# Moving raw weight words, r loads and weight conversion in the first third of an RWKV-7 and hard-swish FFN kernel

## The chip, the cores and the metric

One core of a Trainium2 chip runs the whole program. The metric is the device time of one execution in microseconds (us). PE is the matrix engine, DVE the vector engine, ACT the scalar engine, POOL GpSimd, SP the engine that here only issues DMAs. Each engine works through its own instructions in the order in which the program gives them, and waits where an operand is not ready.

## The reference

Two blocks follow each other. The first is a recurrence over 768 time steps, for 4 batches and 8 heads, with a 40x40 state per head:

```python
y[:, :, t] = einsum('bhd,bhde->bhe', r_t, state)
Sa = einsum('bhde,bhe->bhd', state, a_t)
state = state * w_t[:, :, None, :] - einsum('bhd,bhe->bhde', Sa, b_t) + einsum('bhd,bhe->bhde', v_t, k_t)
```

The second is a feed-forward network (FFN) on the 3072 tokens, each of the 8 x 40 = 320 numbers of y: `h = x @ w_in` (320 to 2048), `g = h * clip(h + 3, 0, 6) / 6`, `out = g @ w_out` (2048 to 320). Inputs of the recurrence are float32. The two weights are float64.

## The kernel before

**The recurrence by blocks.** Time is cut into 12 blocks of 64 steps, batches into two pairs; a block of a pair is a *unit*, 24 in all (`NK`), worked in the order of time, the two pairs in turn. Four units (`NU`) form a *group*. The preparation of a unit (`prepare`) needs no state: products of the decays w (DVE scan L456, reciprocals L467 and L482, copies on POOL L468 to L471), transposes of w, a, b, k on PE (L413), scaled copies, score matmuls masked on DVE (L431, L440), the matrix F of a and b (L505), and KBt on POOL (L549). Then a group's triangular matrices are inverted together (`invert`): a transpose (L607), thirty pairs of a product and an addition on DVE (L619, L625), each needing the one before, and two transposes out (L628, L633); `third_block` (L653 to L680) completes the inverse in `tinv`, the matrix that the diff calls T (128 x 32 x 64 floats, 8 KB in each partition). `step` then carries the state through a unit in named stages: RT and VT (turns of r and v on PE, copied out by ACT, L697 and L729), the scaling of the state (L703 on POOL, L705 on DVE), R (L718, L723), S (L740, L745), U and UT (L756, L777), C and H (score matmuls L431 and masks L440), rS (L793), sn (L811; the state is updated on DVE at L818), y (L834, L846), yg on POOL (L849), and `move` and `move2`, DMAs on SP that lay yg out as the FFN's input xt (L863, L868). Results of PE go through five PSUM banks used in turn, so a stage waits until the bank of five turns ago was read.

**The weights.** PE works in float32, so float64 weights are converted on the chip, in 20 pieces of 1024 raw 32-bit words a partition (`load_weights`). A piece is five DVE instructions (L292, L313, L318, L300, L305) and two of ACT (L294 after L292, L321 after L318). Each `next(weights)` emits one step of this, so what another part of the program asks for sets how densely conversion stands in DVE's order. Raw words need room until they are converted: `raw_homes` lists a home for each piece, in the order of use, and after which piece's conversion a home is free. Homes now are the two halves of the tile `raw` (a, b), two parts of `wout` (c, d) and of `win` (e, f) that are not yet written, and, once the first inversion is over, its tiles `fb`, `tt` and `x`. `limit` says how many pieces may be loaded so far: 2 at the start, 4 and then 12 in the first preparation, all 20 from round 3 on (below). Loads are DMAs on SP (L273).

**The FFN.** For each unit there are two jobs, one for each half of the hidden size. `expand` has 16 matmuls at L914 and 8 at L919 into two PSUM banks `h`, then ACT (L924) and DVE (L925) make two tiles `gt`; `contract` of the job before has 8 matmuls at L938. (Each of these is two matmul records in the trace.) A job is 9 *pieces*, 5 of expand and 4 of contract, and `pieces(n)` emits n of them. A job may be emitted when its xt is there and enough weights are converted (`available`: 10 pieces for the first job of the first two units, else 20).

**The order.** It is written out by hand. First the group 0 is prepared (`by_twos`). Then comes the first inversion, in a loop that lays conversion steps and the first stages of units 0 and 1 between its instructions. Then follow 24 rounds t in which the units 0 to 3 each take one stage a round, beginning at rounds 0, 2, 4 and 10:

```python
for i in range(NU):
    if 0 <= t - begins[i] < len(mine[i]) and mine[i][t - begins[i]]:
        run(chains[i], weight=2.5)
```

`run` emits a stage; at each point where the stage waits for PE, it adds `weight` steps of conversion. From t = 16 on, the preparation of group 1 (`second_group`) runs in the same rounds, with FFN pieces between; the rounds 9 to 15 have one piece each (`FIRST = 9`). After these come 18 turns with 1.25 pieces and the second inversion's instructions. From there the units follow in four blocks each, with FFN pieces at fixed rates, and the rest of the FFN comes last.

**Queues.** `fetch` loads a unit's input, on SP unless an engine is named (L396 for r and v, L399 for the others). `fetch("R", i + 1, ...)` stands after r's turn in the stage RT; ACT issues it for i = 0, 1, 2, SP from then on. ACT also issues the loads of w, a, b and k of unit 5, in rounds 12, 17 and 18.

Of the kernel before, what the change touches and what calls it, by code (L numbers as in the profile page):

```python
# [10 lines left out]
U32 = mybir.dt.uint32  # L11
# [12 lines left out]
def _ap(ap, extra, dims):  # L24

    return bass.AP(tensor=ap.tensor, offset=ap.offset + extra, ap=[list(ap.ap[0])] + dims)
# [3 lines left out]
def kernel(  # L30
# [42 lines left out]
    nc = tc.nc  # L73
# [4 lines left out]
    NU = 2 * NP  # L78
# [84 lines left out]
    def seconds():  # L163
        t = inv.tile([P, 2, H, SLOT], F32, name="WA1", tag="x", bufs=1)
        for i, name in enumerate("WA"):
            others[name] = padded(t[:, i], name)
# [18 lines left out]
    for i in range(3):  # L185
        t = const.tile([P, H, BL], F32, name=f"score{i}")
# [10 lines left out]
    tinv = const.tile([P, NH, BL], F32, name="tinv")  # L197
# [3 lines left out]
    for p in range(NP):  # L201
        t = const.tile([P, 2, NPR, SLOT], F32, name=f"state{p}")
        nc.vector.memset(t[:], 0.0)
        state.append(t)
        t = const.tile([P, 2, NPR], F32, name=f"last{p}")
# [15 lines left out]
    WC = 256  # L221
    PIECES = 20
    converted = [0]
    phase = [0]
    limit, refill = [2], []

    def raw_homes():


        raws = inv.tile([P, NH, BL], F32, name="raw", tag="F", bufs=2)  # L230
        raws = raws[:].rearrange("p h t -> p (h t)").bitcast(U32)
        places = [raws[:, n * 4 * WC:(n + 1) * 4 * WC] for n in range(2)]
        for j in (NJ // 4, 3 * NJ // 4):
            places.append(wout[:, j:j + NJ // 4, :].rearrange("p j m -> p (j m)")[:, 0:4 * WC].bitcast(U32))
        places = [x.rearrange("p (n c t) -> p n c t", n=2, t=2) for x in places]
        for c in (DFF // 4, 3 * DFF // 4):
            x = win[:, :, c:c + 2 * WC].bitcast(U32)
            places.append(x.rearrange("p n (c t) -> p n c t", t=2))
        a, b, c, d, e, f = places
        order = [a, b, c, d, e, f, a, b, c, d, a, b, "fb", "tt", "x", d, a, b, "fb", "tt"]  # L240
        free = [None] * 6 + [0, 1, 2, 3, 6, 7, None, None, None, 9, 10, 11, 12, 13]
        left = {}
        for n, (x, before) in enumerate(zip(order, free)):
            if isinstance(x, str):
                if x not in left:
                    left[x] = inv.tile([P, L, L], F32, name=f"raw_{x}", tag=x)
                x = left[x][:].rearrange("p t s -> p (t s)").bitcast(U32)
                x = x.rearrange("p (n c t) -> p n c t", n=2, t=2)
            yield x, before
# [129 lines left out]
    def fetch(name, i, engine=None):  # L379

        if i is None or i >= NK:
            return
        x, crossed = {"W": (w, 0), "A": (a, 0), "B": (b, 0), "K": (k, 0), "R": (r, 1),
                      "V": (v, 1)}[name]
        if name == "V":
            t = values[i % AHEAD]
        else:
            t = (others if i < 2 * NU and i % 2 and name != "R" else inputs)[name]
        g, p = names[i]
        engine = engine or nc.sync  # L390
        for q in range(2):
            y = x[2 * p + q, :, g * BL:(g + 1) * BL, :]
            rows = slice(q * BL, (q + 1) * BL)
            if crossed:
                for s in range(2):
                    engine.dma_start(out=t[rows, 4 * s:4 * s + 4, 0:D],  # L396
                                     in_=y[s::2].rearrange("h t e -> t h e"))
            else:
                engine.dma_start(out=t[rows, :, 0:D], in_=y.rearrange("h t e -> t h e"))  # L399
        data[i][name + "N"] = t  # L400
# [8 lines left out]
    def turn_pairs(x):  # L409

        o = ps_any([P, NPR, P])
        for n in range(NPR):
            nc.tensor.transpose(out=o[:, n, :],  # L413
                                in_=x[:, 2 * n:2 * n + 2, :].rearrange("p s e -> p (s e)"),
                                identity=ident[:])
        return o

    def turned(name):
        return tmp.tile([P, NPR, P], F32, name=name, tag="turned", bufs=5)
# [168 lines left out]
    def in_turn(stages, order):  # L588

        for name in order:  # L590
            yield from stages[name]()
            shared[0] = None
            yield DONE
# [91 lines left out]
    def step(i):  # L685

        n, o = i % NU, data[i]
        g, p = names[i]
# [4 lines left out]
        def s_RT():  # L693
            x = turn_pairs(o["RN"])
            yield PE
            m["RT"] = turned("RT")
            nc.scalar.activation(out=m["RT"][:], in_=x[:], func=AF.Copy)  # L697
            fetch("R", i + 1, nc.scalar if i < NU - 1 else None)
            if fresh:
                nc.gpsimd.tensor_copy(last_dec[p][:], dec[:, 1])  # L700
                return
            scale = tmp.tile([P, 2, NPR], F32, name="scale", bufs=2)
            nc.gpsimd.tensor_tensor(out=scale[:], in0=last_dec[p][:], in1=dec[:, 0], op=ALU.mult)  # L703
            nc.gpsimd.tensor_copy(last_dec[p][:], dec[:, 1])
            nc.vector.tensor_tensor(out=st[:, :, :, 0:D], in0=st[:, :, :, 0:D],  # L705
                                    in1=_ap(scale[:], 0, [[NPR, 2], [1, NPR], [0, D]]), op=ALU.mult)
# [264 lines left out]
    def pieces(n):  # L971

        owed[0] += n
        while owed[0] >= 1:
            owed[0] -= 1
            if not next(stream):
                owed[0] = 0.0

    def aside(n, weight=0):

        for _ in range(n):
            if side and next(side[0], side) is side:
                side.popleft()
            due[0] += weight
            while due[0] >= 1:
                due[0] -= 1
                next(weights, None)

    def run(stage, steps=0, weight=0, mixed=0):

        for at in stage:
            if at == DONE:
                return
            aside(steps, mixed)
            due[0] += weight
            while due[0] >= 1:
                due[0] -= 1
                next(weights, None)
# [11 lines left out]

    STAGES = 9

    RFETCH, EARLY, FIRST, MIXED = 8, 5, 9, 1 / 3
    TWOS = 14

    def by_twos(first, steps, mixed, rate, fill={}):


        chains = [by_stages(first + i, prepared(first + i)) for i in range(NU)]
        for t in range(TWOS):  # L1020

            order = [0, 1] if t < STAGES else []
            order += [2, 3] if t > 5 else []
            if t == 3:
                order = [2, 3, 0, 1]
            for i in order:
                run(chains[i], steps if t > 10 else 0, fill.get(t, 0), mixed)
                pieces(rate / 2)
            if t == 10:
                side.append(invert(group_F[-1], third, first == 0))  # L1030
            yield
# [4 lines left out]
    for name in "WABK":  # L1036
        for i, engine in enumerate((nc.sync, nc.scalar if name == "W" else nc.sync)):
            fetch(name, i, engine)
    nc.gpsimd.memset(tinv[:], 0.0)
    for t, _ in enumerate(by_twos(0, 4, MIXED, 0, {5: 1, 6: 1, 10: 1})):  # L1040
        if t == 0:
            next(weights)
# [10 lines left out]
    stages = [step(i) for i in range(NU)]  # L1053
    chains = [in_turn(stages[0], ["RT", "VT", "C", "R"]), in_turn(stages[1], ["RT", "VT", "C"])]
    early = deque(chains[i] for i in (0, 0, 1, 1, 0, 1, 0))
    n = 0
    while not third:
        aside(1)
        if not third:
            n += 1  # L1060
            if n % 3 == 1:
                next(weights, None)
            if n % EARLY == 0 and early:
                run(early.popleft())
    assert not early
    while phase[0] in (1, 2, 3):
        next(weights)
    firsts = [third_block(*third[-1], n, True) for n in (0, 2)]
# [18 lines left out]
    chains = [in_turn(stages[i], filter(None, mine[i])) for i in range(NU)]  # L1087
    for t in range(LAST + OWN):
        if t in (1, 3):
            run(firsts[1])  # L1090
        if t == 3:
            limit[0] = PIECES
        for i in range(NU):
            if 0 <= t - begins[i] < len(mine[i]) and mine[i][t - begins[i]]:
                run(chains[i], weight=2.5)
        if t == LAST + 2:
            seconds()
            for name in "WA":
                fetch(name, NU + 1, nc.scalar)
            third.clear()  # L1100
            second_group = by_twos(NU, 3, 0, 1.25)
        if t in (LAST + 7, LAST + 8):

            name = "BK"[t > LAST + 7]
            others[name] = second(name)
            fetch(name, NU + 1, nc.scalar)
        if t >= LAST + 6:
            next(second_group)
        elif t >= FIRST:
            pieces(1)  # L1110
    for _ in weights:
        pass
    for _ in second_group:
# [146 lines left out]
```

## Time and profile before

| | us |
|---|---|
| median of 7 runs | 860.75 |
| lowest and highest | 859.24, 861.36 |
| profiled execution, its own time | 860.93 |
| its span | 859.2 |
| PE busy | 779.5 (91%) |
| PE weight loads busy | 665.9 (78%) |
| DVE busy | 532.1 (62%) |
| ACT busy | 310.8 (36%) |
| POOL busy | 155.9 (18%) |

Busy time is the sum of the stretches in which an engine has an instruction under way; the span is from the first instruction to the last. An engine's share of the whole span says little here, as the stages differ: the preparation and inversion of group 0 fill the first 83 us, the 24 rounds reach to about 191, and from then on PE works nearly without a gap. A wait is put down to the instruction or DMA that ended last before it.

### The profile page before, as it was taken

The numbers are of one execution on the slowest core, as the hardware profiler recorded it, in microseconds if no ns is written. First come the engines' busy times: TensorE is split into PE (matmuls) and PEld (weight loads), VectorE is DVE, ScalarE is ACT, GpSimd is POOL, SyncE is SP. The second block draws the span as 40 slices with busy tenths as digits, with TensorE's granted clock in tenths as the row PEclk, the third lists the DMA queues.
The fourth block names the chain that finished last, engine by engine and source line by source line (L and its number), as shares of the span: only waits on it lengthen the run. The fifth ranks groups of instructions, "written<-read, shape, count | busy, mean of one in ns | idle before, by whom it ended". The sixth has DMA issues, their size and how long they took to land.

```text
span 859.2 us, 34883 instructions
## 1 busy us (share of the span) xinstructions
PE 779.5 (91%) x15480; PEld 665.9 (78%) x15480; DVE 532.1 (62%) x1032; ACT 310.8 (36%) x756; POOL 155.9 (18%) x307
## 2 busy tenths in 40 slices
PE   4723886798999989999999999999999999999998
PEld 3623775686888878888888888888888888888886
DVE  6988797968855569834599553797446774221211
ACT  1323653232354433454423534334353324222211
POOL 4222310212121130220221222113112202000000
PEclk9655578998999998999999999999999999999999
DMA  7571453331123240322232233222132101100000
GB/s 137 86 184 50 111 143 69 57 60 31 30 51 60 48 68 17 62 45 48 45 50 40 44 57 54 46 43 40 37 57 44 26 19 27 27 19 16 14 18 16
DMA packets 174326, 45.00 MB, mean 52 GB/s; under 512 B 157408, under 2 KB 172768, under 8 KB 174176
## 3 DMA queue, kind: packets, MB, share of 16 engines
q1 hardware_dynamic: 165632, 41.46, 25.2%
q8 instruction: 122, 2.00, 1.0%
q10 hardware_dynamic: 8544, 1.31, 1.0%
q14 instruction: 28, 0.23, 0.1%
HBM read 34.08 MB, written 3.93 MB: 44 GB/s over the span
## 4 chain that ended last, share of the span: by engine, by line
PE 79%; DVE 11%; DMA 3%; issue 2%; ACT 2%; SPq 2%; POOL 1%; ACTq 0%; DVEq 0%
PE o L938 25%; PE h L914 20%; PE any L413 6%; PE h L919 6%; PE any L431 3%; PE any L811 3%; PE any L834 3%; PE any L653 2%; PE any L672 2%; DVE prod L619 2%; PE any L756 2%; PE any L718 1%; PE any L576 1%; DVE x L625 1%; SPq L399 1%
## 5 line engine op out<-in xcount | busy, mean ns | idle before, releaser
L938 PE MATMUL o<-wout,gt 128*128 128x320 f32 x768 | 233.0, 450 | 0.0
L914 PE MATMUL h<-xt,win 128*128 128x128 f32 x1536 | 195.1, 281 | 4.9 <-DVE gt L925 4.9
L914 PEld LDWEIGHTS h<-xt,win 128*128 128x128 f32 x1536 | 183.6, 194 | 12.9 <-DVE gt L925 5.0
L938 PEld LDWEIGHTS o<-wout,gt 128*128 128x128 f32 x768 | 141.6, 193 | 55.9 <-issue 2.6
L925 DVE SCALAR_TENSOR_TENSOR gt<-gt,h 128x512 f32<-128x512 f32 x96 | 61.3, 680 | 97.6 <-ACT gt L924 97.6
L924 ACT ACTIVATE gt<-h,three 128x512 f32<-128x512 f32 x96 | 60.7, 683 | 131.5 <-PE h L919 129.0
L849 POOL TENSOR_TENSOR yg<-ys,gam 128x512 f32<-128x512 f32 x24 | 41.4, 1727 | 237.1 <-DVE ys L846 141.0
L619 DVE TENSOR_TENSOR prod<-x 128x30 f32<-128x30 f32 (+9 forms) x180 | 65.8, 365 | 13.6 <-POOL x L610 8.1
L625 DVE TENSOR_TENSOR x<-x,prod 128x30 f32<-128x30 f32 (+9 forms) x180 | 64.3, 357 | 5.3
L549 POOL TENSOR_TENSOR KBt<-K,rgt 128x320 f32<-128x320 f32 x24 | 21.2, 885 | 213.0 <-ACT rgt L541 197.8
L919 PE MATMUL h<-xt,win 64*128 64x128 f32 x768 | 55.8, 285 | 0.0
L440 DVE COPY_PREDICATED score<-mask,any 128x256 f32<-128x256 int32 x143 | 53.1, 435 | 3.9 <-PE any L431 3.9
L919 PEld LDWEIGHTS h<-xt,win 64*128 64x128 f32 x768 | 46.6, 187 | 4.5 <-issue 0.3
L467 DVE RECIPROCAL gam<-prods 128x256 f32<-128x256 f32 x24 | 41.4, 1740 | 13.5 <-POOL yg L849 13.2
L846 DVE TENSOR_TENSOR ys<-any,ys 128x256 f32<-128x256 f32 x44 | 16.6, 419 | 49.6 <-PE any L576 32.3
L482 DVE RECIPROCAL rgam<-prods 128x256 f32<-128x256 f32 x24 | 41.8, 1741 | 0.0
L456 DVE TENSOR_TENSOR_SCAN prods<-wm,start 128x528 f32<-128x528 f32 x24 | 30.1, 1254 | 18.8 <-ACT wm L453 17.1
L697 ACT ACTIVATE RT<-any 128x512 f32<-128x512 f32 x24 | 14.3, 594 | 70.3 <-PE any L413 70.2
L818 DVE TENSOR_TENSOR state<-any,state 128x160 f32<-128x160 f32 x48 | 13.2, 316 | 40.3 <-PE any L431 40.1
L582 ACT ACTIVATE EV<-any 64x160 f32<-64x160 f32 x92 | 24.8, 295 | 33.5 <-PE any L576 19.5
L834 PE MATMUL any<-score,KBt 64*64 64x64 f32 x1536 | 31.0, 229 | 1.7 <-DVE RR L723 0.9
L834 PEld LDWEIGHTS any<-score,KBt 64*64 64x64 f32 x1536 | 27.1, 141 | 6.8 <-issue 3.7
(179 smaller groups left out, 1148.1 us busy)
## 6 DMA issues: line engine op xcount, KB each, us to landing
V<-in_v_dram SPq DMA_DIRECT2D x96, 40.0 KB
out_dram<-ob SPq DMA_DIRECT2D x48, 80.0 KB
B<-in_b_dram SPq DMA_DIRECT2D x46, 80.0 KB
K<-in_k_dram SPq DMA_DIRECT2D x46, 80.0 KB
R<-in_r_dram SPq DMA_DIRECT2D x84, 40.0 KB
W<-in_w_dram SPq DMA_DIRECT2D x40, 80.0 KB
A<-in_a_dram SPq DMA_DIRECT2D x40, 80.0 KB
xt<-yg SPq DMA_DIRECT2D x72, 40.0 KB
```

The source lines that it names most:

```text
L413: nc.tensor.transpose(out=o[:, n, :], in_=x[:, 2 * n:2 * n + 2, :].rearrange("p s e -> p (s e)"), identity=ident[:])
L440: nc.vector.copy_predicated(out=x[:, 4 * i:4 * i + 4, :], mask=mask4, data=o[i])
L467: nc.vector.reciprocal(gv[:, :, 0:HB], o["prods"][:, :, 0, 1:HB + 1][:, :, ::-1])
L482: nc.vector.reciprocal(rv[:, :, HB:BL], o["prods"][:, :, 1, 1:HB + 1])
L619: nc.vector.tensor_tensor(out=pv, in0=_ap(x[:], (i + 1) * L + i, [[L, n], [0, i]]), in1=_ap(x[:], i * L, [[0, n], [1, i]]), op=ALU.mult,)
L625: nc.vector.tensor_tensor(out=rest, in0=rest, in1=pv, op=ALU.add)
L834: nc.tensor.matmul(out=y[q][half(s), pr, :], lhsT=o[name][half(q), h * D:h * D + SLOT], rhs=m[name][half(q), 4 * rs + 2 * s + j, :], start ...
L914: nc.tensor.matmul(out=hp[c][:, i, :], lhsT=win[:, t, j * P:(j + 1) * P], rhs=xt[:, t, :], start=(t == 0 and i == 0), stop=False)
L919: nc.tensor.matmul(out=hp[c][:, i, :], lhsT=win2[half(c), (j0 + i) * P:(j0 + i + 1) * P], rhs=xt[half(c), 2, :], start=False, stop=(i == N ...
L924: nc.scalar.activation(out=gt[:], in_=hp[c][:], func=AF.Relu, bias=three[:], scale=1.0)
L925: nc.vector.scalar_tensor_tensor(out=gt[:], in0=gt[:], scalar=6.0, in1=hp[c][:], op0=ALU.min, op1=ALU.mult)
L938: nc.tensor.matmul(out=op[:], lhsT=gts[c][:, n, :], rhs=wout[:, c * HJ + r * NQ + n, :], start=((split or r == 0) and c == 0 and n == 0), ...
```

## The change

It has five parts:

- The first two pieces' raw words get new homes, g and h, the two halves of T (`tinv`). The memset that clears T moves from the start to the loop of the first inversion, after the second piece is converted. The order of homes and the points at which they come free change with that, and 13 pieces instead of 12 may be loaded before the rounds.
- r of units 2 and 3, and w, a, b and k of unit 5, are loaded by SP instead of ACT. r of unit 1 stays on ACT.
- In the rounds t < 10 a wait on PE brings 1.5 steps of conversion instead of 2.5; from t = 10 on it brings 3.
- `FIRST` becomes 10: rounds 10 to 15 have FFN pieces, not rounds 9 to 15.
- These rounds have two pieces each instead of one.

```diff
         for c in (DFF // 4, 3 * DFF // 4):
             x = win[:, :, c:c + 2 * WC].bitcast(U32)
             places.append(x.rearrange("p n (c t) -> p n c t", t=2))
-        a, b, c, d, e, f = places
-        order = [a, b, c, d, e, f, a, b, c, d, a, b, "fb", "tt", "x", d, a, b, "fb", "tt"]
-        free = [None] * 6 + [0, 1, 2, 3, 6, 7, None, None, None, 9, 10, 11, 12, 13]
+        x = tinv[:].rearrange("p h t -> p (h t)").bitcast(U32)
+        for n in range(2):
+            y = x[:, n * 4 * WC:(n + 1) * 4 * WC]
+            places.append(y.rearrange("p (n c t) -> p n c t", n=2, t=2))
+        a, b, c, d, e, f, g, h = places
+        order = [g, h, a, b, c, d, e, f, a, b, c, d, "x", "fb", "tt", a, b, "fb", "tt", a]
+        free = [None] * 8 + [2, 3, 4, 5, None, None, None, 8, 9, 13, 14, 15]
...
-            fetch("R", i + 1, nc.scalar if i < NU - 1 else None)
+            fetch("R", i + 1, nc.scalar if i == 0 else None)
...
-    RFETCH, EARLY, FIRST, MIXED = 8, 5, 9, 1 / 3
+    RFETCH, EARLY, FIRST, MIXED = 8, 5, 10, 1 / 3
...
-    nc.gpsimd.memset(tinv[:], 0.0)
...
-    n = 0
+    n, cleared = 0, []
     while not third:
         aside(1)
         if not third:
             n += 1
             if n % 3 == 1:
                 next(weights, None)
+            if converted[0] == 2 and not cleared:
+                cleared.append(nc.gpsimd.memset(tinv[:], 0.0))
             if n % EARLY == 0 and early:
                 run(early.popleft())
-    assert not early
+    assert not early and cleared
+    limit[0] = 13
...
-                run(chains[i], weight=2.5)
+                run(chains[i], weight=1.5 if t < FIRST else 3)
         if t == LAST + 2:
             seconds()
             for name in "WA":
-                fetch(name, NU + 1, nc.scalar)
+                fetch(name, NU + 1)
...
-            fetch(name, NU + 1, nc.scalar)
+            fetch(name, NU + 1)
         if t >= LAST + 6:
             next(second_group)
         elif t >= FIRST:
-            pieces(1)
+            pieces(2)
```

## The prediction

> **What bounds the kernel now.** I read the slices of the page first. The columns are 40 equal parts of the span, 21.5 us each.
>
> ```profile
> span 859.2 us, 34883 instructions
> PE   4723886798999989999999999999999999999998
> DVE  6988797968855569834599553797446774221211
> PEclk9655578998999998999999999999999999999999
> ```
>
> Rows are PE and DVE busy in tenths and the granted PE clock. From slice 9 on PE is full at full clock; before that DVE is the fuller engine and PE runs slowly. Nothing after about 200 us can be gained except PE work that was done before. The windows show the stages (us, then busy time of PE, PEld, DVE, ACT, POOL, then clock, DMA share and GB/s):
>
> ```profile
> 82.00:103.00 21.00, 18.41 (x585) 16.84 (x580) 14.31 (x25) 14.40 (x35) 10.01 (x19) 0.58 0.28 69
> 103.00:117.00 14.00, 9.89 (x208) 8.43 (x208) 11.18 (x26) 6.47 (x12) 0.18 (x1) 0.62 0.76 185
> 117.00:157.00 40.00, 28.23 (x568) 24.31 (x567) 32.70 (x55) 17.68 (x38) 7.73 (x16) 0.84 0.40 89
> 157.00:191.00 34.00, 32.34 (x636) 26.62 (x637) 25.29 (x35) 8.93 (x26) 6.38 (x13) 0.95 0.32 54
> 400.00:800.00 400.00, 400.00 (x8172) 342.85 (x8172) 229.29 (x473) 147.52 (x359) 69.38 (x124) 1.00 0.21 39
> ```
>
> From 82 us (end of the first inversion) to 117 PE idles 6.7 us, from 117 to 157 11.8, from 157 to 191 1.7, and none from 400 to 800. So the change is worth what it takes from the 18.5 us of PE idle between 82 and 157, plus the FFN work that it puts there. The waits of 82 to 192 name the owners (total, times, longest):
>
> ```profile
> PE h L914 <- DVE gt L925: 4.9, 1, 4.9
> PE any L718 <- DVE state L705: 3.8, 2, 2.3
> PE any L431 <- DVE state L818: 3.6, 1, 3.6
> ```
>
> All three end on DVE, which works in order and has weight conversion queued ahead of what PE needs. Behind two of DVE's own waits stand DMA issues on ACT, in the timelines of ACT and DVE (start, length, idle before and its releaser):
>
> ```profile
> 104.28 2.85 ACTq L396 DMA_DIRECT2D R<-in_r_dram  x3
> 107.18 0.72 ACT L294 ACTIVATE parts<-parts,low 128x512 uint32<-128x512 uint32 x1 [2.40 <-issue]
> 132.76 1.59 ACTq L399 DMA_DIRECT2D WA<-in_a_dram  x2
> 134.40 0.72 ACT L294 ACTIVATE parts<-parts,low 128x512 uint32<-128x512 uint32 x1 [2.48 <-DVE wout L305]
> ...
> 107.93 0.69 DVE L313 SCALAR_TENSOR_TENSOR parts<-raw,parts 128x512 uint32<-128x512 uint32 x1 [1.83 <-ACT parts L294]
> 138.09 1.29 DVE L925 SCALAR_TENSOR_TENSOR gt<-gt,h 128x512 f32<-128x512 f32 x2 [1.78 <-ACT gt L924]
> ```
>
> **Part 1, raw words in T, and T's memset.** The instruction orders of the two built programs agree on DVE row by row, but for names, up to the two transposes that end the first inversion (79.0 to 82.8 us): cost 0 there. The memset of T (L1039, 1.80 us at 6.55) leaves POOL's start; POOL's next copy idles only 0.18 us, for DVE's scan, so nothing is gained. It returns after the second piece is converted (last read 52.9 us), beside the inversion on DVE. No row shows a large memset beside these. Nearest above: POOL's tensor_tensor at 48.22 (1.04 us), beside which DVE's 108-element product took 0.92 us, while the 108-element add after it took 0.27; at most the whole 1.80 us. Nearest below: the same memset beside the scan of 7.21 us (1.26 us, as the scans alone, 1.24 to 1.28), so 0. I take 0, a memset beside DVE being the nearer row; ends 0 and +1.8.
>
> The Trainium skill ("SBUF — State Buffer", section "SBUF: two separate sides") says that a DVE instruction with two SBUF inputs is locked out only by a GpSimd instruction that reads SBUF. By it the memset costs 0, as I took. By the product's row it would cost up to 1.8.
>
> Pieces 8 to 11 load into homes that come free two conversions later than now. The last, piece 11, waits for the sixth conversion (86.8 us in this trace) and is needed after 105; loads of this size here land within 6 us: cost 0. The tile x, free after 82.8, and limit 13 load piece 12 by about 95, where now pieces 12 and 13 are issued from 93.96.
>
> **Part 2, loads back on SP.** Four batches leave ACT: r of unit 2 (0.60 + 1.97 us at 66.0), r of unit 3 (0.60 + 2.85 us at 103.6), w and a of unit 5 (3.5 us at 130.8), b and k of unit 5 (3.1 us at 150.8). The first held only a copy of v (1.98 us) beside the inversion: worth 0. The next two held L294 for 2.40 and 2.48 us and so DVE for 1.83 and 1.73 us; that of w and a also kept ACT's L924 from starting at 131.1, when PE's L919 had ended, until 137.38, which is PE's 4.9 us. The last held the next L924 by 2.21 us, but DVE came to its half only at 159.8: hidden. On SP an issue takes 0.63 us. r of unit 2 waits there for PE's turn of unit 1 (66.2), with the load of piece 9 behind it, which waits for a conversion of 68.3 anyway. r of unit 3 stands behind the load of piece 14 and waits for PE's turn of unit 2 (100.1), so lands by about 106; needed after 111: cost 0. The loads of unit 5's w and a wait for the tile x, whose piece is converted near 121, and hold the loads of pieces 17 to 19 behind them on SP; piece 17 then lands by 132, needed at about 137. Cost 0 with 5 us to spare; if x were later by more, DVE would wait one for one.
>
> **Part 3, fewer weights in the ten rounds.** The rounds t < 10 hold 16 waits on PE, so 1.5 in place of 2.5 leaves out 16 conversion instructions. A piece is five (0.42 + 0.69 + 0.43 + 0.69 + 0.69 = 2.92 us), so 9.3 us of DVE go behind round 10. Up to 98 us PE is serial (18.4 of 21 us busy at clock 0.58) and gains nothing. Then the wait for L705 goes: ACT no longer has L321 between the unit's results, so POOL's product starts near 99.3, its scale is ready near 101.3, and L718 starts at 102.0, not 104.14. RR (L723) follows PE by one instruction, at 104.1, not 109.0, since neither r's issue nor two conversions stand ahead. The masked score is done at 105.7, not 111.1, and PE goes on to unit 3's turn of r at about 112, not 119.15. Of these 7 us 1.5 are the FFN block (115.85 to 117.4) that FIRST = 10 puts later. Gain at round 10: 5.5 to 7 us.
>
> Now the debt. From the mask of unit 2's C to the state of unit 3 (L818) DVE takes 37.2 us now, with 7 pieces in between. In the new order 8 pieces and one more gt pair (1.29) are there: +2.9 + 1.3 us, less 1.73 (ACT issue) and less part of the wait for L924, about 1: 38.7. The mask ends near 111.5 in place of 119.97. That makes 150; but ACT's wm for the next group, its single tile, and the wait for fb (each 0.8 to 1.9 us in the present row) are also met later relative to the conversions, and I add 3: 153.5, not 157.2. So the gain **shrinks to 3.7 us**. PE's turn after it waits for a PSUM bank that L818 frees, so PE follows.
>
> Behind it two pieces remain (about 3.9 us of DVE), among reciprocals that PE needs. In the order they precede bt and kt; PE had 3 and 5.8 us of slack there now (168.3 to 171.3, 170.2 to 175.9), so they are covered; without that cover, 3.9 us. Where they end, DVE is back at the present order, with the second group's first transpose near 187.5, not 191.24: the same 3.7.
>
> **Part 4, two FFN pieces a round.** At that transpose the new PE order has half an expand more behind it (8 of L914 as coded and 8 of L919: 1.8 + 1.1 us at full clock), and at the last unit's y it is still 8 of L914 ahead (three and a half expands are left, not four; five contracts in both). What is left of FFN after the last recurrence is shorter by this, at full clock and with nothing beside it: **1.8 us**. The fourth job's expand must wait for the third's gt, since the contract that now fills this stretch was done earlier; I count 1 to 2 us of new PE idle near 176, inside the 3.7, because DVE sets the end there.
>
> The sum is made against the profiled execution's own 860.93 us (span 859.2, 1.7 around it; the median of the runs is 860.75): 860.9 - 3.7 - 1.8 = 855.4.
>
> The Trainium skill ("TensorE: Matmul & The Clock Gate", "HAM oscillation") speaks against part 4: idle PE is clocked at half rate. In this trace, after 3.75 us of idle at 195.4, a run of 16 L938 matmuls took 6.05 us, not 4.50. If the wait near 176 did the same, this page's rule would add about 1.5: 856.9.
>
> **Rivals.** (a) The debt is paid in full: DVE sets the pace from round 10, the 3.7 vanish, and only the FFN lead stays, less the possible clock dip: 860.9 - 1.8 = 859.1, to 860.6, call it 859.8. For it: DVE is busy 32.7 of 40 us from 117 to 157. Against it: 3.5 us of its idle there were ACT's issues. (b) Slower: the ten rounds don't shorten, as PE at clock 0.6 is their pace. Then all 9.3 us of conversions move behind round 10; 3.6 come back from ACT's issues and 1.8 from the FFN lead: +3.9, 864.8. It decides from the turn of unit 3's r: if that starts later than about 115.5, the debt is larger than the gain. (c) The ten rounds shorten by 7 and DVE's later waits absorb nearly all of the debt: 860.9 - 7 - 1.8 = 852.1. (d) The homes in T don't do what they say, a load still waiting for the memset: the order has no such wait, and POOL's memset comes after; no chance apart.
>
> **Chances.** Forecast 0.58 (its own range 853 to 858.5; made against the median it would be 855.2), (a) 0.17, (b) 0.15, (c) 0.10. The measurement tells 0.2% (1.7 us) from no change. Faster: 0.58 + 0.10 and a little of (a), 0.71; same: the rest of (a), 0.14; slower: (b), 0.15. The range leaves out (b) and the lower part of (c): 851.5 to 862.5, which takes in the memset's 1.8 and the 3.9 of lost cover on top of the forecast.
>
> **What would show it.** Right: no DMA issue on ACT between 100 and 160; L718 of unit 2 near 102 and the turn of unit 3's r near 112; DVE's L818 of unit 3 near 153.5; the transpose of the second inversion near 187.5; the first inversion's end still at 82.8. Wrong: DVE instructions near 53 us lengthened; DVE waiting for a load of pieces 15 to 19; L818 later than 157; PE idle longer than 3 us between 160 and 200 in places other than that at 195.

## The result, and the profile after

The changed kernel takes **855.91 us** (median of 13 runs, 853.65 to 857.47), the kernel before, run beside it, 860.40 (34 runs). The ratio is 0.9945, with a 95% interval from 0.9936 to 0.9953: 0.55% faster. The prediction was 855.4, in 851.5 to 862.5.

The profiled execution took 853.93 us, 7.0 less than that of before (860.93), while the medians are 4.5 apart: the one is among the short executions of its kernel, the other among the long ones. Some of the difference is there before the change has any say: the first scan began at 6.86 us in place of 7.21, and the transpose tb at the end of the first inversion begins at 78.28 in place of 79.00. Over all executions in the table below but m_copies it begins between 77.75 and 79.00. So 0.7 of the 7.0 us are taken here as a difference between two executions.

Lines from the code behind `raw_homes` are 4 higher in the changed kernel: L914 is now L918, L938 is L942, L818 is L822. The slices of the page, as shown for before:

```profile
span 852.2 us, 34884 instructions
...
PE   4723977898999989999999999999999999999998
...
DVE  7988588979854579743698454697445774222211
...
PEclk8755689799999999999999999999999999999999
```

PE is still nearly full from slice 9 on (slice 10 has 8 tenths, as before); the stages ahead of that changed. The windows (us, busy time of PE, PEld, DVE, ACT, POOL, clock, DMA share, GB/s):

```profile
82.00:103.00 21.00, 18.62 (x582) 16.89 (x580) 10.29 (x20) 13.50 (x34) 8.90 (x18) 0.54 0.43 105
103.00:117.00 14.00, 10.70 (x275) 9.25 (x267) 12.88 (x27) 6.70 (x15) 2.40 (x4) 0.88 0.27 66
117.00:157.00 40.00, 31.40 (x547) 25.30 (x548) 35.25 (x60) 18.46 (x38) 5.60 (x12) 0.86 0.48 104
157.00:191.00 34.00, 31.39 (x655) 26.37 (x654) 27.20 (x37) 10.39 (x28) 7.13 (x14) 0.96 0.28 48
```

From 82 to 157 us PE is busy 60.7 us, before 56.5: the 18.5 us of idle time are 14.3. DVE, from 103 to 157, went from 43.9 to 48.1 of 54 us: its holes are what was filled. From 157 to 191 PE idles 0.9 us more than before, in the waits near 165 and 176. PE's waits between 82 and 192 us (total, times, longest):

```profile
PE h L918 <- DVE gt L929: 2.9, 2, 2.4
PE o L942 <- ACT part L952: 2.5, 1, 2.5
PE any L722 <- DVE state L709: 1.7, 2, 1.5
PE any L435 <- DVE state L822: 1.6, 1, 1.6
```

The wait for gt was 4.9 us and is 2.4 and 0.5; the state's waits (L705 and L818 then) were 3.8 and 3.6 and are 1.7 and 1.6. New is a wait of PE's contract for a copy on ACT, 2.5 us. Six rows of the timelines (start, length) answer to the rows that the prediction named:

```profile
100.79 3.84 SPq L400 DMA_DIRECT2D R<-in_r_dram  x4
...
102.64 0.68 PE L722 MATMUL any<-state,at 40*64 40x40 f32 x32 [0.26 <-DVE state L709]
...
111.12 0.66 PE L417 MATMUL any<-ident,R 128*128 128x128 f32 x4
...
124.73 1.27 SPq L403 DMA_DIRECT2D WA<-in_w_dram  x2
...
153.11 0.55 DVE L822 TENSOR_TENSOR state<-any,state 128x160 f32<-128x160 f32 x2
...
187.94 2.15 DVE L611 STREAM_TRANSPOSE fb<-F 128x1024 f32<-128x1024 f32 x1 [0.39 <-ACT F L515]
```

r of unit 3 and w of unit 5 now leave from SP; no DMA is issued on ACT between 100 and 160 us. Unit 3's r is turned at 111.12 (before 119.15), its state is updated from 153.11 on (before 157.21), the second inversion begins at 187.94 (before 191.24).

One account serves for all runs below. Up to the transpose at the end of the second inversion (tb, L628 or L632) things wait for each other; behind it PE is nearly full (idle for 4.2 to 7.8 us in the executions below), and what is left is mostly PE work. So a span is the time of that transpose plus a rest. The end of the rest is FFN alone: what PE still does behind the last unit's y (L834 or L838) has a column of its own.

| kernel | state of unit 3 | tb | rest | of it, behind the last y | span | ratio to before, 95% interval |
|---|---|---|---|---|---|---|
| before | 157.2 | 225.9 | 633.3 | 41.2 | 859.2 | 1 |
| changed | 153.1 | 220.7 | 631.5 | 39.4 | 852.2 | 0.9945 [0.9936, 0.9953] |
| u_homes: homes as before | 157.4 | 227.3 | 633.0 | 39.4 | 860.3 | 1.0009 [0.9999, 1.0020] |
| u_act: loads on ACT | 155.2 | 223.7 | 631.1 | 39.4 | 854.8 | 0.9974 [0.9961, 0.9986] |
| u_weights: 2.5 everywhere | 157.6 | 225.4 | 632.0 | 37.4 | 857.4 | 1.0007 [0.9996, 1.0018] |
| u_ffn: FFN as before | 150.8 | 226.5 | 632.5 | 41.2 | 859.0 | 1.0016 [1.0006, 1.0027] |
| h_early: no homes in T | 153.0 | 222.9 | 631.2 | 39.4 | 854.1 | 0.9962 [0.9950, 0.9975] |
| f_ten: one FFN piece a round | 150.6 | 221.1 | 635.9 | 42.2 | 857.0 | 0.9982 [0.9973, 0.9990] |
| o_ffn: before + FFN part | 160.9 | 229.7 | 633.4 | 37.4 | 863.1 | 1.0060 [1.0048, 1.0073] |
| o_sp: before + loads on SP | 153.0 | 221.8 | 633.3 | 41.2 | 855.1 | 0.9965 [0.9951, 0.9979] |
| m_copies: POOL copies in T | 164.7 | 233.1 | 631.0 | 39.4 | 864.1 | 1.0071 [1.0050, 1.0091] |
| b_light: weights 1 and 3.5 | 156.0 | 225.1 | 631.4 | 39.4 | 856.5 | 0.9997 [0.9986, 1.0009] |
| b_half: 1.5 FFN pieces | 153.8 | 225.5 | 635.0 | 40.3 | 860.5 | 1.0047 [1.0033, 1.0061] |
| b_three: 3 FFN pieces | 157.6 | 227.1 | 634.0 | 37.4 | 861.1 | 1.0004 [0.9980, 1.0027] |

The first five columns are us of one profiled execution each, the last is of all runs, against the kernel before on the same chip (its medians there: 860.40, then 859.73, 859.37 and 859.97 us). As the profiled execution of before is 0.5 to 1.6 us above these medians, differences of spans are to be read with about that much doubt.

The rest of before, of the changed kernel and of o_ffn, each in two windows, from tb to the end of the last y and from there to PE's last instruction (columns as above, the clock is the last number but two):

```profile
225.90:813.81 587.91, 583.38 (x12212) 500.31 (x12210) 341.52 (x676) 228.09 (x565) 104.44 (x193) 0.99 0.23 41
813.81:854.98 41.17, 41.17 (x273) 33.52 (x272) 5.90 (x10) 5.93 (x10) 1.26 (x1) 1.00 0.06 14
...
220.74:808.61 587.87, 583.64 (x12208) 499.29 (x12207) 339.60 (x676) 228.20 (x565) 105.47 (x193) 1.00 0.23 41
808.61:847.99 39.38, 39.38 (x257) 31.73 (x256) 5.90 (x10) 5.94 (x10) 1.27 (x1) 1.00 0.06 14
...
229.70:821.43 591.73, 584.19 (x12198) 500.06 (x12194) 340.74 (x676) 227.58 (x565) 105.58 (x193) 0.99 0.22 41
821.43:858.83 37.40, 37.40 (x241) 29.87 (x240) 5.90 (x10) 5.94 (x10) 1.27 (x1) 1.00 0.06 15
```

In the first of the two windows the granted clock was 0.50 for 6.83 us in before and for 3.41 in the changed kernel. u_homes has the FFN order of the changed kernel and 6.83 us at 0.50; its window takes 589.4 us and its rest 633.0. So differences of the rest of up to 1.7 us can be the clock of one execution.

### The profile page after: what moved, and what is told of

It reads as the page before. It is cut to its first block, busy times and chain, and to the rows that moved or that the text cites. A ratio compares the mean times of both kernels' runs of the same rounds, so it can differ in the third digit from the quotient of the medians.

```text
span 852.2 us, 34884 instructions
## 1 busy us (share of the span) xinstructions
PE 777.7 (91%) x15480; PEld 661.6 (78%) x15480; DVE 529.6 (62%) x1032; ACT 310.2 (36%) x756; POOL 156.8 (18%) x307
## 4 chain that ended last, share of the span: by engine, by line
PE 79%; DVE 12%; issue 2%; ACT 2%; DMA 1%; POOL 1%; SPq 0%; DVEq 0%; ACTq 0%
PE o L942 24%; PE h L918 20%; PE h L923 6%; PE any L417 6%; PE any L435 4%; PE any L815 3%; PE any L838 3%; PE any L676 2%; PE any L657 2%; PE any L760 2%; PE any L722 2%; DVE prod L623 1%; PE any L580 1%; DVE x L629 1%; PE any L797 1%
## 5 line engine op out<-in xcount | busy, mean ns | idle before, releaser
L942 PE MATMUL o<-wout,gt 128*128 128x320 f32 x768 | 235.2, 449 | 2.5 <-ACT part L952 2.5
L918 PE MATMUL h<-xt,win 128*128 128x128 f32 x1536 | 196.7, 282 | 2.9 <-DVE gt L929 2.9
L918 PEld LDWEIGHTS h<-xt,win 128*128 128x128 f32 x1536 | 185.1, 195 | 12.1 <-DVE gt L929 3.8
L942 PEld LDWEIGHTS o<-wout,gt 128*128 128x128 f32 x768 | 139.3, 191 | 56.6 <-ACT part L952 2.7
L822 DVE TENSOR_TENSOR state<-any,state 128x160 f32<-128x160 f32 x48 | 13.3, 318 | 58.7 <-PE any L435 54.6
L460 DVE TENSOR_TENSOR_SCAN prods<-wm,start 128x528 f32<-128x528 f32 x24 | 30.1, 1254 | 17.1 <-ACT wm L457 16.2
L701 ACT ACTIVATE RT<-any 128x512 f32<-128x512 f32 x24 | 14.3, 596 | 59.7 <-PE any L417 59.7
L727 DVE TENSOR_TENSOR RR<-any,EV 128x160 f32<-128x160 f32 x44 | 12.2, 318 | 30.7 <-PE any L435 30.7
L838 PE MATMUL any<-score,KBt 64*64 64x64 f32 x1536 | 29.4, 225 | 0.2 <-DVE RR L727 0.2
```

Source lines behind the costliest of these rows:

```text
L838: nc.tensor.matmul(out=y[q][half(s), pr, :], lhsT=o[name][half(q), h * D:h * D + SLOT], rhs=m[name][half(q), 4 * rs + 2 * s + j, :], start ...
L918: nc.tensor.matmul(out=hp[c][:, i, :], lhsT=win[:, t, j * P:(j + 1) * P], rhs=xt[:, t, :], start=(t == 0 and i == 0), stop=False)
L942: nc.tensor.matmul(out=op[:], lhsT=gts[c][:, n, :], rhs=wout[:, c * HJ + r * NQ + n, :], start=((split or r == 0) and c == 0 and n == 0), ...
```

## The experiments: each part taken back

Each of the four takes one part of the change back and leaves the others.

**u_homes.** The homes, limits and the place of the memset are those of before.

```diff
-        order = [g, h, a, b, c, d, e, f, a, b, c, d, "x", "fb", "tt", a, b, "fb", "tt", a]
+        order = [a, b, c, d, e, f, a, b, c, d, a, b, "fb", "tt", "x", d, a, b, "fb", "tt"]
...
-    limit[0] = 13
```

> The changed kernel with the old homes, limits and memset of T at the start; loads on SP, 1.5 and 3 steps and two FFN pieces a round stay. Theory (homes alone give nothing): 0 to +1.5 us over the changed kernel's 855.9, since the w and a of unit 5 now wait on SP for the tile x, which holds piece 14 and not piece 12, and so land near 137, when PE wants them. Rival (the homes carry the gain, by earlier loads or by the memset gone from the start): +3 or more, and DVE waiting for a load.

Measured 860.31 us: the whole gain is gone. The timelines of SP and PE of this run, around the first FFN matmul:

```profile
97.70 0.81 SPq L273 DMA_DIRECT2D raw<-in_moe_w_in_dram  x2
99.55 3.42 SPq L396 DMA_DIRECT2D R<-in_r_dram  x4
...
106.00 2.78 SPq L273 DMA_DIRECT2D raw_x<-in_moe_w_in_dram  x4
110.26 4.13 SPq L863 DMA_DIRECT2D xt<-yg  x4
...
117.08 2.26 PE L914 MATMUL h<-xt,win 128*128 128x128 f32 x9 [6.43 <-DMA xt<-yg]
```

SP stood 28.3 us at the load that starts at 97.70, whose home a late conversion had to free; then r of unit 3 and the loads of four pieces went out one after the other, and only behind them, at 110.26, the transfers of unit 0's y to xt. The y was there at 100.2, when POOL's yg ended. PE waited 6.4 us for xt. In the changed kernel the same transfers start at 104.72. The queue that the prediction called free of cost is free only if the homes come free early enough for what stands behind the loads.

**u_act.** The loads of r and of unit 5's inputs are on ACT as before.

```diff
-            fetch("R", i + 1, nc.scalar if i == 0 else None)
+            fetch("R", i + 1, nc.scalar if i < NU - 1 else None)
...
-                fetch(name, NU + 1)
+                fetch(name, NU + 1, nc.scalar)
```

> The changed kernel with r of units 2 and 3 and w, a, b, k of unit 5 issued by ACT again. Theory (issues on ACT hold DVE and the gt tiles): +3 to +4 us, most of it from w and a, whose 3.5 us of issue would stand ahead of the first gt activation at 125. Rival (the issues are hidden, ACT being only 36% busy): +0 to +1.

Measured 857.53 us, 0.9974: 0.3% of the 0.55% are gone, about 2.5 us where 3 to 4 were expected. PE's wait for gt is 3.8 us in place of 2.4, and unit 3's state is 2.1 us later.

**u_weights.**

```diff
-                run(chains[i], weight=1.5 if t < FIRST else 3)
+                run(chains[i], weight=2.5)
```

> The changed kernel with 2.5 steps of conversion in all rounds. Theory: the turn of unit 3's r goes back from 111 to about 116, but the conversions end earlier, so the state of unit 3 comes 1 to 2.5 us later than in the changed kernel: 857 to 858.5. Rival (where the conversions stand doesn't matter, DVE has the same sum): within 0.5 us of 855.9.

Measured 860.12 us, 1.0007: all of the gain is gone, a loss of 5.3 us where 1 to 2.5 were expected. Unit 3's state falls back to 157.6.

**u_ffn.** One piece a round from round 9, weights still changing at round 10.

```diff
-    RFETCH, EARLY, FIRST, MIXED = 8, 5, 10, 1 / 3
+    RFETCH, EARLY, FIRST, MIXED = 8, 5, 9, 1 / 3
...
-                run(chains[i], weight=1.5 if t < FIRST else 3)
+                run(chains[i], weight=1.5 if t < 10 else 3)
...
-            pieces(2)
+            pieces(1)
```

> The changed kernel with one FFN piece in rounds 9 to 15 (1.5 steps still for t below 10). Theory: the FFN lead of 8 matmuls of the first layer goes, so +1.8 us: 857.7. Rival (the second piece only brings new waits, on gt and on the bank o, that eat its lead): 855.9 or less.

Measured 860.73 us, 1.0016: slower than before, where 1.8 us were expected. Unit 3's state is the earliest but one of all runs (150.8), and yet the second inversion begins 2.9 us later than in the changed kernel. DVE's timeline (start, length, idle before and its releaser):

```profile
153.44 0.68 DVE L929 SCALAR_TENSOR_TENSOR gt<-gt,h 128x512 f32<-128x512 f32 x1
157.84 0.69 DVE L929 SCALAR_TENSOR_TENSOR gt<-gt,h 128x512 f32<-128x512 f32 x1 [3.72 <-ACT gt L928]
...
190.81 2.17 DVE L611 STREAM_TRANSPOSE fb<-F 128x1024 f32<-128x1024 f32 x1 [3.41 <-ACT F L515]
```

DVE stood 3.7 us at a gt pair, because ACT could not write the next gt tile until PE's contract had read the one before (ACT waited 4.7 us for L942): at one piece a round the contract is spread over rounds, and DVE's next reciprocal, which the preparation of group 1 needs, stands behind the pair. Another 3.4 us went at the transpose itself, for F.

The four together: taking back one part costs 2.5 to 6 us each, 19 us in sum, and all of them gave 4.5. **The parts are not terms of a sum.**

## The experiments: parts alone, and the cause of each loss

**h_early.** T is no home and is cleared at the start; the inversion's tiles hold pieces 10 to 12.

```diff
-        order = [g, h, a, b, c, d, e, f, a, b, c, d, "x", "fb", "tt", a, b, "fb", "tt", a]
-        free = [None] * 8 + [2, 3, 4, 5, None, None, None, 8, 9, 13, 14, 15]
+        order = [a, b, c, d, e, f, a, b, c, d, "x", "fb", "tt", a, b, d, "fb", "tt", a, b]
+        free = [None] * 6 + [0, 1, 2, 3, None, None, None, 6, 7, 9, 11, 12, 13, 14]
...
```

> The new kernel with T out of it again (memset of T at the start, six homes, as before), but with the tiles x, fb and tt, which come free at the end of the first inversion, as homes of pieces 10 to 12 rather than 12 to 14. Theory A: what the old homes cost was SyncE's queue: a piece load stood there until 97.7 us for its home's conversion, and the loads of four pieces behind it (8 issues, 5.5 us, with r of unit 3) went out only then and pushed the transfers of unit 0's y to xt from 104.7 to 110.3 us, so PE stood 6.4 us at the first FFN matmul. With x, fb and tt loading from about 86 us that wait is gone and the time is that of the new kernel within 1.5 us: 854.5 to 857.5. Theory B: the two more homes in T are themselves the gain (two more pieces ahead, or the memset off the start): 859 to 861.

Measured 856.02 us, 0.9962. Most of what u_homes lost is back, with no word in T; the transfers to xt start at 104.08, and PE does not wait for them. So it was SP's queue, and theory A holds; what T's two homes add beyond that is 0.17% by the middle values, and the intervals touch, so whether they add anything is open.

**f_ten.** As the changed kernel, with `pieces(1)`.

> The new kernel with one FFN piece a round in place of two; FIRST stays 10. Theory A: at one piece a round a contract is not through when the next job's gelu on ScalarE needs its gt buffer, and VectorE stands behind that gelu (3.7 us at 157 us with FIRST 9), while PE has less to do between its waits: 859 to 862, with a wait of over 3 us of VectorE for the gelu between 150 and 175 us, and more PE idle from 117 to 191 us than the 11.2 us of the new kernel. Theory B: what cost was the start in round 9, an FFN block ahead of a unit's recurrence: then this one is 855 to 857.

Measured 857.81 us, between the two theories. DVE's long stop for gelu near 157 is gone, and tb is at 221.1, as good as in the changed kernel; but the rest is 4.4 us longer: 2.9 of them are FFN work left behind the last y, and what remains can be the clock (0.50 for 6.83 us between tb and that y, not 3.41). PE idles 11.4 us from 117 to 191, hardly more than the 11.2 of the changed kernel, against theory A. The start in round 9 cost some 3 us (u_ffn against f_ten), the halved rate another 3 (f_ten against the changed kernel).

**o_ffn.** The kernel before with `FIRST` 10 and `pieces(2)`, nothing else.

> The kernel before with the FFN part alone: FIRST 10 and two pieces a round. Theory A, the prediction's: the FFN lead is a term of its own, 8 of L914 fewer behind the last unit's y, 1.8 us: a ratio of 0.998, 858 us. Theory B: the parts work only together: VectorE, still with 2.5 weights a step and held by ScalarE's issues, takes the gelu pairs of the earlier FFN work in front of unit 3's state, so what the lead gives at the end comes back there: a ratio of 0.9995 to 1.003.

Measured 865.00 us, 1.0060: 5.6 us slower, beyond both theories, on the side of B. PE still waits 5.2 us at 134 us for gt, whose gelu stands behind ACT's issues of w and a (130.08 to 132.81); two gt pairs, not one, stand in front of unit 3's state, which comes 3.7 us later than before, at 160.9. The FFN work behind the last y is 3.8 us shorter, but the stretch from tb to that y is 3.8 us longer, with 3.0 us more of PE idle in it, so the rest stays (633.4).

**o_sp.** The kernel before with the loads on SP, nothing else.

> The kernel before with the loads on SyncE alone; homes, weights and FFN as before. Theory A, the prediction's: ScalarE's two batches go (1.83 and 1.73 us of VectorE and the gelu that PE waited 4.9 us for), so unit 3's state is 2 to 4 us earlier and the time 0.996 to 0.998. Theory B: with the old homes the same issues stand in SyncE's queue ahead of the transfers of unit 0's y, PE waits for xt, and nothing is gained or up to 3 us lost: 0.9995 to 1.004.

Measured 856.57 us, 0.9965: theory A. This one part alone gives 2.8 of the 4.5 us. The old homes do no harm here: the transfers of unit 0's y go out at 108.93, 4.2 us later than in the changed kernel, but PE comes to its first FFN matmul only at 113.67 and does not wait for them.

**m_copies.** T's memset is followed by copies of one half of T into the other, all zeros.

```diff
                 cleared.append(nc.gpsimd.memset(tinv[:], 0.0))
+                for _ in range(14):
+                    nc.gpsimd.tensor_copy(tinv[:, 0:NH // 2], tinv[:, NH // 2:NH])
```

> The new kernel with 14 GpSimd copies of one half of T into the other (128x1024 each, zeros onto zeros, so that nothing computed changes) right behind T's memset, beside the inversion on VectorE. A memset reads nothing, a copy reads SBUF. Theory A (the Trainium skill's rule on GpSimd and VectorE, as the prediction cited it): only the copies lock out VectorE's instructions with two SBUF inputs: the products and adds from 54 us on last longer than in the new kernel (0.33 to 0.41 us there) while copies run, and the first inversion ends later, by 3 us or more; the time is 3 to 12 us over the new kernel's: 859 to 868. Theory B: GpSimd beside VectorE costs nothing here, reading or not: durations as before, the inversion's transpose at 78.3 us as in the new kernel, time 855 to 857.

Measured 865.89 us, 1.0071: theory A. The timelines of POOL and DVE in this run:

```profile
51.88 1.81 POOL L1067 MEMSET tinv<- 128x2048 f32 x1 [2.99 <-DVE win L309]
...
53.00 0.35 DVE L623 TENSOR_TENSOR prod<-x 128x184 f32<-128x184 f32 x1
...
53.75 16.21 POOL L1069 COPY tinv<-tinv 128x1024 f32<-128x1024 f32 x14
...
55.09 1.08 DVE L623 TENSOR_TENSOR prod<-x 128x198 f32<-128x198 f32 x1
...
57.21 1.26 DVE L322 TENSOR_SCALAR raw<-raw 128x512 uint32<-128x512 uint32 x1
```

Beside the memset a product takes 0.35 us; beside the copies the next sizes take 1.08, and even DVE's one-input instruction (L322, 0.42 us otherwise) takes 1.26. The end of the first inversion moves from 78.28 to 88.98. In the changed kernel, with the memset alone:

```profile
52.20 1.81 POOL L1067 MEMSET tinv<- 128x2048 f32 x1 [3.29 <-DVE win L309]
...
52.96 0.33 DVE L629 TENSOR_TENSOR x<-x,prod 128x168 f32<-128x168 f32 x1
53.32 0.35 DVE L623 TENSOR_TENSOR prod<-x 128x184 f32<-128x184 f32 x1
```

The instructions beside it last as long as those around it. So the memset cost nothing. A copy beside the inversion cost about 0.76 us for each 1.16 us that it ran (10.7 us for 16.2).

**b_light.** `weight=1 if t < FIRST else 3.5`.

> The new kernel with weights 1 in the ten rounds and 3.5 behind (1.5 and 3 in the new one). Theory A, the prediction's debt: what is left out ahead of round 10 is met between the mask of unit 2's C and unit 3's state and behind it, so the state moves by under 1 us, the last conversions reach the reciprocals behind it, and the time is 855.5 to 859. Theory B: each conversion instruction that leaves the ten rounds is worth as much as the first 16: 852 to 854.5.

Measured 859.27 us, 0.9997: theory A in direction, and larger: unit 3's state is 2.9 us later, where under 1 was expected. From DVE's and PE's timelines:

```profile
91.83 0.56 DVE L822 TENSOR_TENSOR state<-any,state 128x160 f32<-128x160 f32 x2 [6.00 <-PE any L815]
...
101.00 0.49 DVE L709 TENSOR_TENSOR state<-state,scale 128x320 f32<-128x320 f32 x1 [3.00 <-POOL scale L707]
...
125.00 2.07 PE L918 MATMUL h<-xt,win 128*128 128x128 f32 x8 [5.58 <-DVE gt L929]
```

DVE idles 6.0 us at 91.8 (3.9 in the changed kernel) and 3.0 at 101.0 (there 1.6, at the instruction before): what left these rounds had been hidden in waits that PE and POOL set. The next scaling of a state is 3.3 us earlier for it (113.4, not 116.7), but then the debt comes, and PE waits 5.6 us for gt at 125 in place of 2.4.

**b_half and b_three.** 1.5 and 3 FFN pieces a round.

> The new kernel with 1.5 FFN pieces a round from round 10 (2 in the new one, 1 in the run that gave 0.9982). Theory A: the gelu pairs that the FFN work brings ahead of unit 3's state cost VectorE about 2.5 us at 2 pieces, and what pays for them is PE work done before the second inversion ends; at 1.5 both are about half: 855.5 to 857.5, unit 3's state between 150.6 and 153.1 us. Theory B: an optimum between the two: 853 to 855.

> The new kernel with 3 FFN pieces a round from round 10. Theory A: one more gelu pair or none comes ahead of unit 3's state, since each job's expand needs the transfer of a y that the recurrence delivers; PE has no more idle time there that FFN work could take, and the state is later by 0 to 2 us: 855.5 to 859. Theory B: the FFN lead goes on paying 1.8 us a half expand: 853 to 855.

Measured 863.88 us (1.0047) and 861.14 (1.0004): all four expectations missed. With 1, 1.5, 2 and 3 pieces the ratio goes 0.9982, 1.0047, 0.9945, 1.0004. In b_half unit 3's state is at 153.8, 0.7 us behind the stretch that was expected; PE waits 4.0 us for gt at 130, 4.3 for the state at 154 and 2.8 at 164 for ACT's copy of the bank `o`, and the rest is 3.5 us longer than in the changed kernel. In b_three the state is 4.5 us later, though two gt pairs stand ahead of it, as in the changed kernel. The FFN work left behind the last y falls with the rate, as it should (42.2, 40.3, 39.4 and 37.4 us). It is the stretch from tb to that y that does not follow it: 589.5, 590.6, 587.9 and 592.5 us, with 4.5, 5.8, 4.2 and 7.8 us of PE idle. The runs show which waits each rate meets; why the one at 2 pieces meets the fewest is open. No run was faster than the changed kernel.

## Why the prediction was right, point by point

**Part 1, homes and memset: the memset right at 0,** shown by the durations beside it and by their contrast with the copies. The new homes cost nothing, as predicted, but they are not worth nothing: beside the other parts the old ones lose 5.5 us (u_homes). The Trainium skill's rule ("SBUF — State Buffer", "SBUF: two separate sides"), which the prediction weighed, holds on both sides here: the memset, which reads nothing, cost 0, the copies 10.7 us. The upper end of 1.8 us, taken from a product beside POOL's tensor_tensor, was a row of a reading instruction and had no bearing.

**Part 2, loads on SP: right that SP costs nothing with the new homes, and that ACT's issues held DVE and PE.** The prediction let 1.73 us and about 1 us of it into its debt, and r's issue into its gain at round 10. o_sp, which changes only this, has the state 3.5 us earlier, counted from tb of the first inversion (74.76 us behind it, not 78.21); taken back from the changed kernel (u_act) it is 1.7 us (76.50, not 74.83). Its reason for zero cost on SP looked at when the loads land; that unit 0's transfers to xt stand in the same queue was not looked at, and u_homes shows that this costs 6.4 us of PE wait when four pieces' loads go ahead of them.

**Part 3, fewer weights: the times were right, the shares not.** L722 starts at 102.64 (predicted 102.0), RR is at 104.54 (104.1), the mask at 105.33 (done at 105.7 predicted, at 106.1 measured), the turn of unit 3's r at 111.12 (112), unit 3's state at 153.11 (153.5), the transpose at 187.94 (187.5). Part by part at unit 3's state, counted in the same way: loads on SP -3.5 (before to o_sp), fewer weights with the homes and FIRST 10 another -2.7 (o_sp to f_ten), two pieces a round +2.8 (f_ten to the changed kernel). This sums to -3.4; -3.7 was predicted. The shares hold in this order only: each taken back from the changed kernel, the loads are worth 1.7 us at the state, the weights 4.9 (u_weights), and the FFN part costs 1.8 (u_ffn). So the sum was right and its split cannot be tested; but in both orders the FFN work ahead of the state costs more than the one gt pair (1.3 us) that was counted. The debt was sized well: from the mask of unit 2's C (done at 112.11) to the state DVE takes 41.0 us, where before it took 37.2 and the prediction had 38.7 plus 3 (its 111.5, 38.7 and 3 make 153.2, not the 153.5 that it went on with). That the debt grows with fewer weights ahead is shown by b_light.

**Part 4, two FFN pieces: 1.8 us as predicted, but not as a term of its own.** Behind the last y PE works 39.38 us, not 41.17: the 8 matmuls of L914 that were counted, for 1.8 us. That the whole rest is 1.8 shorter too (631.5, not 633.3) is in part luck: at equal clock the FFN order gains 0.3 us there (u_homes, 633.0, against before) or 1.0 (the changed kernel against u_ffn, 632.5). And the term does not say what else the edit does: alone (o_ffn) it leaves 37.40 us behind the last y and yet loses 5.6 us, as the state comes later and PE idles more ahead of that y. The edit paid only where the other parts were made too. The 1 to 2 us of new PE idle near 176 are 0.5 and 0.6; not foreseen were the 2.4 us at 126.7 for gt and the 2.5 at 148.65, where a contract waits until ACT has copied the last one out of the single bank `o`, with ACT held by the decay copies and DVE.

Between the transpose fb and tb the changed kernel gains another 1.9 us (32.8 in place of 34.7) that the prediction did not have: four gt instructions fall into the second inversion on DVE, not six (1.3 us). 3.3 us at fb, 0.7 of the start among them, and 1.9 here are 5.2 at tb, and 1.8 behind it make the 7.0 of the profile. Against the medians' 4.5, the predicted 5.5 is therefore about as good as a sum from one execution can be. Part of its closeness is luck: at fb the gain is 2.6 us without the difference of the start, where 3.7 was predicted, and the 1.9 us behind fb, which the prediction did not have, make up for that.

**Rivals.** (a) asked that the gain at the state be lost; it is 3.4 us. (b) asked that unit 3's r turn later than 115.5; it turns at 111.12. (c) asked for 3 us more. u_weights, u_ffn and b_light show how near (a) was: tb as before within 1 us, ratio within 0.2% of 1, though only b_light comes to it by a debt, as (a) said.

## What to carry to other kernels

Moving work between stages that share in-order queues had no price per part here: three of four parts, taken back alone, each lost the whole gain or more, and one of them, made alone, lost 5.6 us; so measure the parts alone and all but one before crediting any. When a load goes to a queue, list what stands behind it there, transfers of results as well as loads, and ask when the load's own buffer comes free. On POOL, clear a buffer beside DVE's work (here 0 us), but do not copy there (here 10.7 us for 14 copies).

## What the runs showed of the hardware

**A short gap can halve PE's clock.** Windows of the changed kernel around two waits of PE, idle from 124.28 to 126.71 us and from 146.15 to 148.65 (columns as above):

```profile
121.91:125.32 3.41, 2.37 (x64) 1.96 (x60) 2.68 (x7) 1.73 (x4) 0.71 (x3) 1.00 0.29 45
125.32:128.74 3.42, 2.03 (x43) 1.85 (x44) 2.74 (x5) 1.19 (x3) 0.00 (x0) 1.00 0.65 109
145.80:149.21 3.41, 0.91 (x6) 0.59 (x4) 3.38 (x5) 1.59 (x4) 2.13 (x4) 1.00 0.37 63
149.21:152.62 3.41, 2.67 (x9) 1.51 (x8) 3.38 (x4) 0.00 (x0) 0.00 (x0) 0.50 0.42 65
152.62:156.04 3.42, 2.56 (x36) 2.24 (x37) 3.42 (x7) 1.57 (x4) 0.00 (x0) 0.50 0.51 83
156.04:159.45 3.41, 3.41 (x10) 2.35 (x9) 3.38 (x5) 0.36 (x2) 0.00 (x0) 0.50 0.67 116
159.45:162.86 3.41, 3.41 (x67) 2.57 (x69) 2.56 (x5) 0.95 (x3) 0.00 (x0) 1.00 0.15 27
```

After 2.5 us of idle the granted clock is 0.50 from 149.2 to 159.4 us; a run of four L942 takes 2.34 us at 155.4, and 1.24 at 140.2, at full clock. The Trainium skill ("TensorE: Matmul & The Clock Gate", "HAM oscillation") names about 3.4 us as the gap from which this happens. The measurement decides: 2.5 us was enough here, while 2.4 us at 126.7 was followed by full clock. In the traces of all runs the granted clock changes only at points that lie whole multiples of 3.41 us apart. The second wait fell into one such stretch, in which PE was busy for 0.91 us; the first lay across two, with 2.37 and 2.03 us. That the busy part of a stretch alone decides is not shown: 2.08 us from 114.86 on in u_act were followed by 0.50.

**One program, ten microseconds.** Twelve executions of b_three took 854.02 to 863.84 us; the two shortest (854.02 and 854.26) had a mean granted clock of 0.943, the three longest (863.09 to 863.84) 0.934 to 0.938. In its profiled execution (862.94) the clock is 0.50 from 153.0 to 173.4 us. The changed kernel's 13 runs spread over 3.8 us. That the clock is the cause, and not the waits that lower it, is not shown.

**POOL's copy against DVE.** Fourteen copies of 128x1024 took 16.2 us beside DVE, 1.16 us each, and DVE's instructions beside them 1.08 to 1.52 us each (0.34 to 0.69 us otherwise), as if each had waited for a copy to end. That wait shows as a longer instruction, not as idle time.
